# Retention attention and a routed expert layer on one core: 4096-byte x pieces, 512 KB weight loads, and a new deal of the front, the selections and the last steps

## The chip, the cores and the metric

One NeuronCore of a Trainium2 chip runs the whole program. The metric is device time in microseconds (us), the median of several executions.

## The reference

```
# attention: B=4, H=8, S=768, D=64, float32
for t in range(S):
    state = gamma * state + k[:, :, t] (outer) v[:, :, t]
    y[:, :, t] = scale * q[:, :, t] @ state
x = y as (B*S = 3072 tokens, H*D = 512)
# experts: 4 groups of 4, w1 (512, 1024) and w2 (1024, 512) each, float32
g_idx = argmax(x @ w_group);  e_idx = argmax(x @ w_expert[g_idx])
out[token] = softmax(g)[g_idx] * softmax(e)[e_idx] * relu(x @ w1[g, e]) @ w2[g, e]
```

Every token goes to one of 16 experts, which one is known only after its attention row is done.

## The kernel before

**The attention stage** runs 12 steps (i = 0 to 11), each with two batches of 128 tokens. A step has the score products of queries and keys (`score_mm`, into PSUM banks sh0 to sh3), the causal mask on VectorE (`score_mask`, tile pf), the product with the carried state (`state_out`), the product of pf with the scaled values (`value_out`; the scaling, tile vs, is `vprep` on GpSimd), the state update (`state_mm`, copied to V by ScalarE), the transposes of the next step's keys (`keys_mm`), and on VectorE the decay factors (`out_x`: xt = op * gx). The token logits of step i - 1 (`logits_mm`, copied to ls by ScalarE), the transposes of its xt into rows (`trans_mm`, copied to xr and written to the DRAM tensor xd), and the selection product that brings the logits into the bank log (line 326) come one step later. The scores of step i + 1 are made in step i, so that TensorE always has something between a product and its mask.

**Routing** (`route`) is a chain of some twenty small VectorE instructions for each four blocks of 128 tokens: maxima, one-hots (oh), a TensorE product that counts the ranks (lines 399 and 401), list slots and weights (src). GpSimd then scatters the token numbers into the experts' lists in DRAM (`enlist`, tensor meta). After the last step the order of the experts by load is computed (`order`, tile ord).

**The expert stage.** Experts 0 and 1 have an early list from the first half of the tokens; ua and va are those passes, ub and vb the rest of the same experts, us[0] to us[13] the other fourteen. A pass reads its list (tile mt), gathers rows of xd (tile xg), transposes them (`xtrans`, line 658), and splits x and the float32 weights wf into a float16 part and a bfloat16 rest: wh on ScalarE and wl on VectorE (`wsplit`, lines 616 and 618), xbh and xbl likewise. The first layer's products (line 681) go to banks hps, which `hh` (ScalarE) and `hl` (VectorE, line 689) empty, the second's (line 713) to yps. Early weight pieces of ua are split on GpSimd and ScalarE during the attention stage.

**What sets the order.** The program is written in its order by hand: the schedule is manual, each engine executes its instructions in the order in which the Python code records them, and the calls `beside(i, place)` and `extra(i)` put expert work into the attention steps. SyncE issues nearly all loads from one queue, in order. `NEXT` says which weight pieces of va are loaded at which step, `KEYED` which steps get their key rows by a load instead of transposes. Ahead of step 0, `attention` loads what a string names: q, k, v with a step number (A and B are halves), d for the decay table gx, w for the routing weights.

The lines that the change touches and what calls them:

## Time and profile before

| | us |
|---|---|
| median of 3 runs | 426.81 |
| lowest and highest | 423.11, 432.28 |
| profiled execution | 427.34 |
| its span in the trace | 425.6 |

The span runs from the first instruction to the end of the last write; the profiled execution's own time is 1.7 us above it. The profile page gives each engine's busy time; TensorE (PE) is busy for 404.0 us. Times in the rows further on are us from the span's start.

### The profile page before, as it was taken

How to read it: one execution, taken by the hardware profiler on the slowest of the kernel's cores; microseconds unless marked ns; L12 is line 12 of the kernel's file. 1: busy time of each engine (PE TensorE's matmuls, PEld its weight loads, DVE VectorE, ACT ScalarE, POOL GpSimd, SP SyncE). 2: the span in 40 equal slices, each digit the busy share in tenths (PEclk: the TensorE clock that was granted, in tenths of full speed). 3: DMA queues.
4: the chain of work that ended last, by engine and by line, in shares of the span. 5: the costliest groups of instructions: out<-in, count | busy, mean ns of one | idle time of the engine just before them, and what ended most of it. 6: DMA issues, size and time to landing. Idle time of an engine off the chain costs nothing.

```text
span 425.6 us, 13495 instructions
## 1 busy us (share of the span) xinstructions
PE 404.0 (95%) x5692; PEld 332.4 (78%) x5721; DVE 290.1 (68%) x473; ACT 222.8 (52%) x342; POOL 175.9 (41%) x153
## 2 busy tenths in 40 slices
PE   8899999999798999999999999999999999999991
PEld 4789888787675768585979788897978878879791
DVE  4455585578892557776889786867768777787620
ACT  2135336446541556646556665665766657667520
POOL 4445669748877022340508142351513405222001
PEclk9999999999999999999999999999999999999996
DMA  8999999997536867776776786978788797896001
GB/s 282 378 313 327 373 306 339 336 285 243 161 94 236 333 220 249 245 258 235 257 246 214 259 277 239 315 246 283 266 286 284 272 306 270 280 327 233 27 9 34
DMA packets 36913, 107.94 MB, mean 254 GB/s; under 512 B 13784, under 2 KB 13784, under 8 KB 29684
## 3 DMA queue, kind: packets, MB, share of 16 engines
q1 hardware_dynamic: 25908, 89.76, 61.9%
q0 software_dynamic: 10944, 17.31, 11.7%
q8 instruction: 45, 0.74, 0.7%
q14 instruction: 16, 0.13, 0.1%
HBM read 94.65 MB, written 13.77 MB: 255 GB/s over the span
## 4 chain that ended last, share of the span: by engine, by line
PE 58%; issue 26%; POOL 6%; DMA 4%; DVE 2%; SPq 1%; ACT 0%; POOLq 0%; DVEq 0%; ACTq 0%
PE hps L681 19%; PE yps L713 8%; PE yps L759 6%; PE yps L761 5%; PE op L291 5%; POOL out L814 4%; PE sh L227 3%; POOL xg L640 2%; PE op L278 2%; DMA gx<-dec 2%; PE sh L322 2%; PE tpx L658 2%; PE stp L253 2%; PE sh L310 2%; PE sh L212 1%
## 5 line engine op out<-in xcount | busy, mean ns | idle before, releaser
L618 DVE TENSOR_TENSOR wl<-wf,wh 128x1024 bf16<-128x1024 f32 x120 | 148.5, 1248 | 40.0 <-ACT wh L616 35.4
L681 PE MATMUL hps<-xbh,wh 128*128 128x128 f16 (+14 forms) x576 | 134.2, 245 | 0.9 <-ACT xr L329 0.9
L681 PE MATMUL hps<-xbl,wh 128*128 128x128 bf16 (+14 forms) x576 | 134.2, 245 | 0.3 <-issue 0.3
L616 ACT ACTIVATE wh<-wf 128x1024 f16<-128x1024 f32 (+1 forms) x136 | 133.5, 1002 | 1.8 <-DMA wf<-w1p 1.8
L681 PE MATMUL hps<-xbh,wl 128*128 128x128 f16 (+14 forms) x576 | 134.2, 245 | 0.1
L814 POOL DMA_INDIRECT out<-yo,mt x32 | 41.3, 1289 | 180.4 <-ACT yo L796 152.7
L681 PEld LDWEIGHTS <-wh 128*128 128x128 f16 x1152 | 102.5, 98 | 4.7 <-issue 1.9
L640 POOL DMA_INDIRECT xg<-xd,mt x32 | 52.5, 1641 | 26.3 <-DMA mt<-meta 17.4
L686 ACT ACTIVATE hh<-hps 128x256 f16<-128x256 f32 (+14 forms) x72 | 35.1, 488 | 52.3 <-PE hps L681 51.5
L761 PEld LDWEIGHTS <-wh 128*128 128x128 f16 x704 | 44.7, 98 | 21.0
L681 PEld LDWEIGHTS <-wl 128*128 128x128 bf16 x576 | 56.3, 98 | 1.1 <-issue 0.5
L239 DVE TENSOR_TENSOR pf<-sh,cst 128x512 f32<-128x512 f32 x48 | 30.8, 685 | 30.0 <-PE sh L227 10.3
L689 DVE SCALAR_TENSOR_TENSOR hl<-hps,hh 128x256 bf16<-128x256 f32 (+14 forms) x69 | 38.1, 553 | 16.7 <-ACT hh L686 14.2
L660 ACT ACTIVATE xbh<-tpx 128x512 f16<-128x512 f32 (+13 forms) x32 | 16.9, 527 | 47.2 <-PE tpx L658 47.1
L661 DVE TENSOR_TENSOR xbl<-tpx,xbh 128x512 bf16<-128x512 f32 (+13 forms) x32 | 19.2, 601 | 21.5 <-ACT xbh L660 21.5
L440 POOL DMA_INDIRECT meta<-src,slot x24 | 27.6, 1151 | 14.3 <-DVE src L394 7.1
L759 PE MATMUL yps<-wh,hh 128*128 128x512 f16 x88 | 33.4, 380 | 0.0
L759 PE MATMUL yps<-wh,hl 128*128 128x512 f16 x88 | 33.4, 379 | 0.0
L187 POOL TENSOR_TENSOR vs<-lv,cst 128x512 f32<-128x512 f32 x24 | 24.6, 1047 | 20.8 <-DMA lv<-qkv 10.9
L761 PEld LDWEIGHTS <-wl 128*128 128x128 bf16 x352 | 23.1, 98 | 10.4
L761 PE MATMUL yps<-hh,wl 128*128 128x103 f16 (+10 forms) x352 | 26.3, 197 | 1.2
L761 PE MATMUL yps<-hl,wh 128*128 128x103 bf16 (+10 forms) x352 | 26.3, 197 | 0.0
(146 smaller groups left out, 600.0 us busy)
## 6 DMA issues: line engine op xcount, KB each, us to landing
wf<-w1p SPq DMA_DIRECT2D x26, 1024.0 KB
wf<-w2p SPq DMA_DIRECT2D x26, 1024.0 KB
xd<-xr SPq DMA_DIRECT2D x12, 512.0 KB
lq<-qkv SPq DMA_DIRECT2D x11, 512.0 KB
lk<-qkv SPq DMA_DIRECT2D x11, 512.0 KB
lv<-qkv SPq DMA_DIRECT2D x11, 512.0 KB
wf<-w1p SPq DMA_DIRECT2D x16, 256.0 KB
wf<-w2p SPq DMA_DIRECT2D x16, 256.0 KB
```

The lines of the kernel that those rows point to most:

```text
L239: nc.vector.tensor_tensor(o, sc, tri, ALU.mult)
L440: i = nc.gpsimd.indirect_dma_start(out=self.metaf, out_offset=bass.IndirectOffsetOnAxis(ap=slot[:, c:c + 1], axis=0), in_=src[:, c, :], in ...
L616: nc.scalar.activation(u["wh"][i][:, cs], u["wf"][i][:, cs], AF.Copy)
L618: (eng or nc.vector).tensor_tensor(u["wl"][i][:, cs], u["wf"][i][:, cs], u["wh"][i][:, cs], ALU.subtract)
L640: nc.gpsimd.indirect_dma_start(out=xg[0:r, i, :], out_offset=None, in_=self.xd[0:n, :], in_offset=bass.IndirectOffsetOnAxis(ap=mt[0:r, i, ...
L681: nc.tensor.matmul(hv[:, a, 0:W], l[:, k, fs], r[:, k, 0:W], start=(n == 0), stop=(n == 11))
L686: nc.scalar.activation(hh[:, f, 0:W], hv[:, :, 0:W], AF.Relu)
L689: nc.vector.scalar_tensor_tensor(*rest)
L713: nc.tensor.matmul(ps[0:r, :], l[:, k, ts], m[k], start=(n == 0), stop=(n == 23))
L759: nc.tensor.matmul(big, h[:, k, 0:P], w[k], start=(n == 0), stop=(n == 23))
L761: nc.tensor.matmul(yv[:, d, 0:r], w[k][:, d * P:d * P + P], h[:, k, P:P + r], start=(n == 0 and d == 0), stop=(n == 23), skip_group_check= ...
L814: s = nc.gpsimd.indirect_dma_start(out=self.out, out_offset=bass.IndirectOffsetOnAxis(ap=mt[0:r, i, 0:1].bitcast(U32), axis=0), in_=yo[0:r ...
```

## The change

- The constants cst are loaded in two parts: 308 columns (masks and decay) at once and the remaining 263 (tile rest, routing constants) after the front loads. In the load string the decay table and v of step 1 come ahead of q and k of step 2.
- In steps 0 and 1 the scores of the next step are put behind `out_x`, and the keys of the next step are transposed into the bank log and sh0 instead of sh0 and sh1.
- A step's rows of x lie together in xd (token 256 i + 2 p + u), so xr goes out as 128 pieces of 4096 bytes instead of 256 of 2048; the host puts the output rows back in their order. Weight pieces of ua and va are 128 by 1024 (512 KB) instead of 128 by 512.
- The selection product is a function of its own, and in the steps whose keys are not transposed it is put off into the next step (`select_late`).
- The last steps: the last logits go to a bank of their own (tag sta), xr of the last step has its own buffer, one wl of va precedes the last route instead of four, three follow the held `hl` and stand ahead of `order`; the routing weights of the last route come ahead of its ranks; ua's fourth hps bank has the tag tra; xg1 is zeroed by ScalarE instead of GpSimd; in step 10 `vprep` precedes the gathers.
- `listed` has a new argument for the engine that reads the lists; no call gives it, so SyncE still reads them.

```diff
-NEXT = {9: (0, 4), 10: (4, 8), 11: (8, 12)}
+NEXT = {(9, 0): (0, 1), (9, 3): (1, 2), (10, 0): (2, 4), (11, 0): (4, 6)}
...
-    def logits_mm(self, i, bank):
+    def logits_mm(self, i, bank=None):
 
         nc, s = self.nc, self.st[i]
-        lt = self.sh[bank][:, 0:2 * P]
+        lt = self.pp.tile([P, 512], F32, name="lgt", tag="sta", bufs=1) if bank is None else self.sh[bank]
+        lt = lt[:, 0:2 * P]
...
-    def trans_mm(self, i):
+    def select_mm(self, i):
+
+        nc, s = self.nc, self.st[i]
+        for u in range(2):
+            a = LG + 20 * (i % 2 * 2 + u)
+            lg = self.log[:, a:a + 20]
+            nc.tensor.matmul(lg, s["ls"][:, u * P:u * P + P], self.rest[:, C_SEL:C_SEL + 20], start=True, stop=True)
+
+    def select_late(self):
+        if self.late is not None:
+            self.select_mm(self.late)
+            del self.st[self.late]
+            self.late = None
+
+    def trans_mm(self, i, pool=None, late=False):
 
         nc, s = self.nc, self.st[i]
...
-        for u in range(2):
-            a = LG + 20 * (i % 2 * 2 + u)
-            lg = self.log[:, a:a + 20]
-            nc.tensor.matmul(lg, s["ls"][:, u * P:u * P + P], self.cst[:, C_SEL:C_SEL + 20], start=True, stop=True)
-        xr = self.wp.tile([P, 2, DM], F32, name="xr", bufs=1)
+        if not late:
+            self.select_mm(i)
+        xr = (pool or self.wp).tile([P, 2, DM], F32, name="xr", bufs=1)
         for u in range(2):
             nc.scalar.activation(xr[:, u], self.sh[2 + u], AF.Copy)
-        g, c = divmod(i, NC)
-        xd = self.xd.rearrange("(b r) f -> r b f", r=S)[c * P:c * P + P, 2 * g:2 * g + 2, :]
-        nc.sync.dma_start(xd, xr)
+        xd = self.xd[2 * P * i:2 * P * i + 2 * P, :].rearrange("(p u) f -> p (u f)", u=2)
+        nc.sync.dma_start(xd, xr.rearrange("p u f -> p (u f)"))
...
+        if last:
+            yield from weights()
         yield "wait"
...
         if not last:
             yield "wait"
-        yield from weights()
+            yield from weights()
...
-        for o in "qB0 kB0 vA0 vB0 q1 k1 q2 k2 v1 d0 w0".split():
+        for o in "qB0 kB0 vA0 vB0 q1 k1 d0 v1 q2 k2 w0 c0".split():
             n, us = int(o[-1]), {"A": (0,), "B": (1,)}.get(o[1], (0, 1))
             if o[0] == "d":
                 self.decay_load()
+            elif o[0] == "c":
+                self.nc.sync.dma_start(self.rest, self.a_cst[:, C_REST:])
             elif o[0] == "w":
...
-            beside(i, -1)
             if not last:
                 self.vprep(i + 1)
+            beside(i, -1)
             if i == 3:
...
             if i:
-                scores(i + 1, 0)
+                if i > 1:
+                    scores(i + 1, 0)
+                if not last:
+                    self.select_late()
                 if i % 2 == 0:
                     self.route_steps(99, True)
                 self.state_out(i, 0)
+                self.select_late()
                 self.state_out(i, 1)
-                scores(i + 1, 1)
+                if i > 1:
+                    scores(i + 1, 1)
...
-            if i == 0:
-                scores(1, 0)
-                scores(1, 1)
             self.out_x(i)
+            if i < 2:
+                scores(i + 1, 0)
+                scores(i + 1, 1)
             if last:
                 self.route_steps(1, True)
             beside(i, 1)
             if not last:
-                self.keys_mm(i + 1)
+                self.keys_mm(i + 1, banks=(self.log, self.sh[0]) if i < 2 else None)
                 self.load("k", i + 4)
             if i:
-                self.trans_mm(i - 1)
-                del self.st[i - 1]
+                late = i + 1 in KEYED or i % NC == NC - 2
+                self.trans_mm(i - 1, late=late)
+                if late:
+                    self.late = i - 1
+                else:
+                    del self.st[i - 1]
...
+            ua["banks"] = ["big"] * 3 + ["tra"]
...
                 if place == 0:
                     if 2 <= i <= 9:
-                        for k in range(2):
-                            self.wload_part(ua, 2 * i - 4 + k)
-                    for k in range(*NEXT.get(i, (0,))):
-                        self.wload_part(va, k)
+                        self.wload_part(ua, i - 2)
                     if i == 10:
                         self.wsplit(va, 0, low=False)
-                        self.wsplit(va, 1, low=False)
-                    if last:
-                        self.wsplit(va, 0, high=False)
                 if place == 2:
                     if last:
-                        self.xtrans(ua, 'big', (0,))
-                        self.wsplit(va, 2, low=False)
+                        self.xtrans(ua, 'big', (0,), low=False)
+                        self.wsplit(va, 1, low=False)
                 if place == 1:
                     early(i - 1, 0, False)
                     if last:
-                        self.wsplit(va, 3, low=False)
+                        self.xlow(ua, 0)
+                if place == 3:
+                    if last:
+                        self.wsplit(va, 2, low=False)
...
-            nc.gpsimd.memset(self.xg[1], 0.0)
 
             last = NS2 - 1
-            self.logits_mm(last, 3)
-            for k in (1, 2, 3):
-                self.wsplit(va, k, high=False)
-            first(2)
-            self.trans_mm(last)
-            for k in range(12, 16):
+            self.logits_mm(last)
+            self.wsplit(va, 0, high=False)
+            self.trans_mm(last, self.yp)
+            for k in (6, 7):
                 self.wload_part(va, k)
             while self.todo:
                 self.enlist(*self.todo.pop(0))
...
             route = self.route(len(BATCHES) - 1)
             while next(route) != "wait":
                 pass
-            self.wsplit(va, 4, low=False)
-            self.wsplit(va, 5, low=False)
             self.held = []
             first(4)
+            self.wsplit(va, 3, low=False)
             next(route)
-            first(2)
+            first(4)
             for _ in route:
                 pass
             while self.todo:
...
             for h in self.held:
                 nc.vector.scalar_tensor_tensor(*h)
             self.held = None
-            self.xtrans(va)
+            self.xtrans(va, "sta")
+            for k in range(2):
+                nc.scalar.activation(self.xg[1][:, k], self.one, AF.Copy, scale=0.0)
+            self.wsplit(va, 4, low=False)
+            self.wsplit(va, 5, low=False)
             self.listed(ub)
             self.listed(vb)
+            for k in (1, 2, 3):
+                self.wsplit(va, k, high=False)
             self.steps.append(self.order())
             self.route_steps(99)
             assert not self.steps
-            self.wsplit(va, 4, high=False)
-            self.wsplit(va, 5, high=False)
+            for k in (4, 5):
+                self.wsplit(va, k, high=False)
```

Where it moves instructions. SyncE, the loads of the front, before:

```order
L177 DMA lq<-qkv 128x1024
L177 DMA lk<-qkv 128x1024
L177 DMA lq<-qkv 128x1024
L177 DMA lk<-qkv 128x1024
L177 DMA lv<-qkv 128x1024
L190 DMA gx<-dec 128x512
L879 DMA wr<-wr 128x4x20
```

and now:

```order
L178 DMA lq<-qkv 128x1024
L178 DMA lk<-qkv 128x1024
L191 DMA gx<-dec 128x512
L178 DMA lv<-qkv 128x1024
L178 DMA lq<-qkv 128x1024
L178 DMA lk<-qkv 128x1024
L904 DMA wr<-wr 128x4x20
L902 DMA rest<-cst 128x263
```

The decay table gx has moved ahead of q and k of step 2 and of v of step 1, v of step 1 ahead of q and k of step 2, and the second part of the constants behind wr.

TensorE at the end of the attention stage (log<-..,ls is the selection; sh the logits or the transposes of x; lgt the new bank), before:

```order
L322 MATMUL sh_108<-ident,xt 128x128 x4
L322 MATMUL sh_109<-ident,xt 128x128 x4
L326 MATMUL log<-cst,ls 128x20 x2
L310 MATMUL sh_109<-xt,wr 32x256 x4
L681 LDWEIGHTS wh
L681 MATMUL hps<-xbh,wh 128x128
```

and now:

```order
L338 MATMUL sh_110<-ident,xt 128x128 x4
L325 MATMUL log<-rest,ls 128x20 x2
L312 MATMUL lgt<-xt,wr 32x256 x4
L338 MATMUL sh_109<-ident,xt 128x128 x4
L338 MATMUL sh_110<-ident,xt 128x128 x4
L325 MATMUL log<-rest,ls 128x20 x2
L704 LDWEIGHTS wh
```

The last logits leave bank sh_109, into which the transposes just ahead of them were written, and the first layer of ua no longer stands between them and the last transposes and selection.

VectorE around the last route (r, slot: ranks to list slots; ex, eg, u, src: weights), before:

```order
L390 TENSOR_SCALAR u<-log 128x4
L392 SCALAR_TENSOR_TENSOR log<-log,u 128x4
L394 RECIPROCAL src_129<-log 128x4
L430 TENSOR_SCALAR rows_2147<-nb 1x1
L430 TENSOR_SCALAR rows_2149<-nb 1x1
L1081 SCALAR_TENSOR_TENSOR hl<-hps,hh 128x2x128 x3
L661 TENSOR_TENSOR xbl<-tpx,xbh 128x4x128
L461 TENSOR_TENSOR cnt<-nb,cst 1x16
L465 SCALAR_TENSOR_TENSOR key<-cnt,cst 1x16
L467 MEMSET key 1x1
```

and now:

```order
L425 TENSOR_TENSOR nb<-log,nb 128x16
L429 TENSOR_TENSOR r_2120<-log,oh 128x64
L431 TENSOR_REDUCE log<-r_2120 128x4
L434 CAST slot<-log 128x4
L445 TENSOR_SCALAR rows_2125<-nb 1x1
L445 TENSOR_SCALAR rows_2127<-nb 1x1
L1113 SCALAR_TENSOR_TENSOR hl<-hps,hh 128x2x128 x4
L683 TENSOR_TENSOR xbl<-tpx,xbh 128x4x128
L633 TENSOR_TENSOR wl<-wf,wh 128x1024 x3
L476 TENSOR_TENSOR cnt<-nb,rest 1x16
L480 SCALAR_TENSOR_TENSOR key<-cnt,rest 1x16
```

The weights have gone ahead of the ranks, all four hl are held until behind the route instead of three, and three wl of va, which stood ahead of the last route, now stand between it and `order` (cnt, key).

## Rows read from the trace of the kernel before

**Rows 1.** The profile page: the span, and each engine's busy time, share of the span and instructions.

```profile
span 425.6 us, 13495 instructions
PE 404.0 (95%) x5692; PEld 332.4 (78%) x5721; DVE 290.1 (68%) x473; ACT 222.8 (52%) x342; POOL 175.9 (41%) x153
```

**Rows 2.** Table of stretches, TensorE's granted clock and all engines; columns: stretch in us from the span's start, its length, busy time (and instructions) of PE, its weight loads PEld, DVE, ACT and POOL, granted clock, share of the DMA engines, GB/s. The rows: the front (steps 0 and 1), step 10, the end of attention with the first layer of ua, the fourteen other experts, the last write.

```profile
2.50:25.50 23.00, 20.82 (x404) 16.38 (x402) 11.12 (x21) 5.40 (x11) 11.27 (x16) 1.00 0.98 362
91.50:100.70 9.20, 8.53 (x184) 7.00 (x180) 8.19 (x19) 4.49 (x8) 4.16 (x4) 1.00 0.92 325
106.40:117.20 10.80, 7.63 (x121) 6.98 (x122) 9.43 (x28) 5.42 (x11) 9.45 (x8) 1.00 0.53 160
159.10:418.70 259.60, 256.01 (x3054) 212.53 (x3078) 189.85 (x233) 156.57 (x217) 82.26 (x53) 1.00 0.71 242
418.70:425.60 6.90, 0.00 (x0) 0.00 (x0) 0.00 (x0) 0.00 (x0) 0.00 (x0) 0.50 0.10 38
```

**Rows 3.** Timeline of the front and of step 2 (25.51 to 33.69) on TensorE, and of two other engines in the front; columns: start, time taken, engine, line, operation, output<-input, shapes, count, and in brackets the engine's idle time ahead of it and what ended it.

```profile
7.79 0.90 PE L227 MATMUL sh<-lq,lk 64*64 64x128 f32 x32 [0.67 <-DMA lk<-qkv]
12.36 1.57 PE L227 MATMUL sh<-lq,lk 64*64 64x128 f32 x64
17.57 0.40 PE L278 MATMUL op<-lq,V 64*64 64x128 f32 x2 [0.66 <-DVE xt L303]
25.51 0.90 PE L227 MATMUL sh<-lq,lk 64*64 64x128 f32 x32
...
31.43 1.09 PE L212 MATMUL sh<-ident,lk 128*128 128x128 f32 x8
33.69 0.90 PE L227 MATMUL sh<-lq,lk 64*64 64x128 f32 x32
...
16.00 2.04 POOL L187 TENSOR_TENSOR vs<-lv,cst 128x512 f32<-128x512 f32 x2 [5.52 <-DMA lv<-qkv]
13.33 2.48 DVE L239 TENSOR_TENSOR pf<-sh,cst 128x512 f32<-128x512 f32 x4 [3.29 <-PE sh L227]
16.73 1.29 DVE L303 TENSOR_TENSOR xt<-op,gx 128x512 f32<-128x512 f32 x2 [0.92 <-DMA gx<-dec]
```

**Rows 4.** DMA over the stretch 12 to 22, in which nearly all packets carry 4096 bytes, and under it over 100 to 118, in which nearly all large ones carry 2048; columns: queue, packets, MB, share of the 16 engines' time.

```profile
q1 hardware_dynamic: 1604, 3.71, 98.4%
...
q1 hardware_dynamic: 1540, 2.90, 55.2%
```

**Rows 5.** Timeline of TensorE in step 4, at the end of step 8 and at the end of step 10.

```profile
44.62 0.58 PE L227 MATMUL sh<-lq,lk 64*64 64x64 f32 x16 [0.80 <-issue]
82.18 0.62 PE L326 MATMUL log<-cst,ls 128*128 128x20 f32 x4 [0.21 <-ACT ls L315]
100.16 0.62 PE L326 MATMUL log<-cst,ls 128*128 128x20 f32 x4 [0.22 <-ACT ls L315]
```

**Rows 6.** Timeline of TensorE from the end of step 11 to the second layer of va.

```profile
107.35 0.64 PE L310 MATMUL sh<-xt,wr 128*32 128x256 f32 x8 [0.97 <-ACT xr L329]
112.91 0.22 PE L681 MATMUL hps<-xbh,wh 128*128 128x128 f16 x1 [0.90 <-ACT xr L329]
115.73 0.20 PE L399 MATMUL log<-oh,stri 128*128 128x80 bf16 x1 [1.32 <-DVE oh L374]
122.83 0.22 PE L681 MATMUL hps<-xbh,wh 128*128 128x128 f16 x1
128.19 0.38 PE L713 MATMUL yps<-wh,hh 128*128 128x512 f16 x1
132.53 0.66 PE L658 MATMUL tpx<-ident,xg 128*128 128x128 f32 x4 [1.58 <-DMA xg<-xd,mt]
```

**Rows 7.** Timeline of VectorE over the same stretch.

```profile
98.36 3.39 DVE L618 TENSOR_TENSOR wl<-wf,wh 128x1024 bf16<-128x1024 f32 x1
108.68 4.61 DVE L618 TENSOR_TENSOR wl<-wf,wh 128x1024 bf16<-128x1024 f32 x3
113.55 0.23 DVE L358 TENSOR_REDUCE m<-log 128x20 f32<-128x80 f32 x1
115.46 0.22 DVE L374 TENSOR_TENSOR oh<-log,go 128x64 bf16<-128x64 f32 x1
118.22 0.18 DVE L394 RECIPROCAL src<-log 128x4 f32<-128x4 f32 x1
122.83 2.35 DVE L618 TENSOR_TENSOR wl<-wf,wh 128x1024 bf16<-128x1024 f32 x2
125.10 0.42 DVE L689 SCALAR_TENSOR_TENSOR hl<-hps,hh 128x256 bf16<-128x256 f32 x1
```

**Rows 8.** Timeline of GpSimd over the same stretch (vs is the scaling of values; meta a scatter to the lists, xg a gather).

```profile
96.17 1.08 POOL L640 DMA_INDIRECT xg<-xd,mt  x1 [6.63 <-DMA mt<-meta]
98.62 2.05 POOL L187 TENSOR_TENSOR vs<-lv,cst 128x512 f32<-128x512 f32 x2
112.19 1.95 POOL L440 DMA_INDIRECT meta<-src,slot  x1 [0.30 <-PE hps L681]
114.45 0.98 POOL L440 DMA_INDIRECT meta<-src,slot  x1 [0.30 <-issue]
122.98 1.93 POOL L440 DMA_INDIRECT meta<-src,slot  x1 [0.30 <-DVE ord L490]
129.08 1.05 POOL L640 DMA_INDIRECT xg<-xd,mt  x1 [2.88 <-DMA mt<-meta]
```

More of the change, by code (lines that the diff above doesn't have):

```diff
@@ L340, in route @@
         c0, n = BATCHES[i]
-        cst = self.cst
+        cst = self.rest
         def t(name, *shape, dt=F32):
@@ L451, in order @@
     def order(self):
-        nc, rp, cst = self.nc, self.rp, self.cst
+        nc, rp, cst = self.nc, self.rp, self.rest
         V = nc.vector
@@ L494, in items @@
     def items(self):
-        nc, rp, cst = self.nc, self.rp, self.cst
+        nc, rp, cst = self.nc, self.rp, self.rest
         V = nc.vector
@@ L618, in wsplit, with listed @@
             (eng or nc.vector).tensor_tensor(u["wl"][i][:, cs], u["wf"][i][:, cs], u["wh"][i][:, cs], ALU.subtract)
-    def listed(self, u, group=None):
+    def listed(self, u, group=None, eng=None):
         nc, tc, bp = self.nc, self.tc, self.bp
@@ L670, in layers @@
         for f2 in range(4):
-            ps = pp.tile([P, 512], F32, name="hps", tag="big", bufs=3)
+            tag = u.get("banks", ["big"] * 4)[f2]
+            ps = pp.tile([P, 512], F32, name="hps", tag=tag, bufs=3 if tag == "big" else 1)
             hv = ps.rearrange("p (a t) -> p a t", a=2)
@@ L952, in attention @@
                 self.route_steps(99, True)
+            if i == 1:
+                self.nc.vector.tensor_copy(self.stri, self.rest[:, C_STRI:C_STRI + P])
             entries(4 if last else 2 if i in (8, 10) else 1)
@@ L1017, in beside @@
                 last = i == NS2 - 1
+                for k in range(*NEXT.get((i, place), (0,))):
+                    self.wload_part(va, k)
                 if place == -1 and i == 10:
@@ L1200 @@
     r = run_bass_kernel_spmd(nc, [arrays], core_ids=[0])
-    return r.results[0]["out"]
+    out = r.results[0]["out"].reshape(B // 2, NC, P, 2, DM)
+    return np.ascontiguousarray(out.transpose(0, 3, 1, 2, 4)).reshape(NT, DM)
```

49 lines of the change are left out of this document (28 added, 21 removed).

## Prediction

> **What bounds the kernel now.** I read the busy times first, then the table of stretches, then the waits of TensorE. [...] In the fourteen late experts it idles 3.6 of 259.6 us, and the change leaves their order alone, so that stretch keeps its length; the 6.9 us of the last write stay too. What can be had lies ahead of 136 us: 2.2 idle us in the front, 0.7 in step 10, 3.2 between 106.4 and 117.2 [rows 2], 1.58 at the gather of ub [rows 6]. A busy TensorE is not always a working one: matmuls held up inside a group count as busy. So I price stretches by comparing one with another that does the same work.
>
> **The front.** Step 2 runs from 25.51 to 33.69, 8.18 us, without a named wait. The stretch from 12.36 to 25.51, 13.15 us, has the same work plus one more pair of scores (1.57) and one more set of key transposes (1.09): 10.84 us. So 2.3 us are lost there, of which the trace names 0.66, the wait for `out_x`, which itself waits for the decay table until 16.73 [rows 3]. In the new order of loads 1 MB (q and k of step 2, 128 x 1024 x 4 bytes each) and v of step 1 (0.52 MB) no longer stand ahead of the table: 1.57 MB at the 377 GB/s that a stretch of 4096-byte packets reached (3.71 MB in 98.4% of 10 us) [rows 4] are 4.2 us, so it lands near 12.5, when value_out of step 0 has just ended. v of step 1 comes 1.05 MB less 0.26 MB earlier, 2.1 us: its scaling starts at 13.9 instead of 16.00 [rows 3], and value_out of step 1, which now stands ahead of the next scores, needs it only near 15.7. What is late next are the masks: `out_x` (1.29) now precedes them on VectorE, and sh0, sh2 and sh3 come free one mask (0.62, from 2.48 for four) [rows 3] after another; I count 0.4 us of such waits, from 0 to 1.2. The bank log for the first key transposes takes away the wait for sh0 at no cost, since the selection comes 2 us later. The constants shrink by 263 of 571 columns, 135 KB, 0.36 us at that rate, in front of the load for which TensorE waits 0.67 us at 7.79 [rows 3]: 0.36. The sum of the front is 2.3 - 0.4 + 0.36, **2.3 us**, from 1.0 (the named 0.66 and 0.36 alone) to 2.7.
>
> **Late selections.** At the ends of steps 8 and 10 the selection waits 0.21 and 0.22 us for ls [rows 5]. Put off behind the next scores or half of `state_out`, it finds ls ready: **0.4 us**, from 0 to 0.4. Its consumer, the route's first maximum, still stands behind masks.
>
> **The end of attention.** I keep the clock of before. TensorE is through with the selection of step 10 at 106.38 (107.35 less 0.97) [rows 6]. The last logits now have their own bank, so the 0.97 goes; logits (0.64), transposes (1.09 as for keys) [rows 3] and selection end near 108.6, and 48 products of ua's first layer follow, half of the 5.36 us that va's 96 take from 122.83 to 128.19 [rows 6]: 111.3. The 0.90 at 112.91, for xr that waited for its last write, goes with the new buffer.
> VectorE comes free at 108.68. Before, three wl (4.61) stood ahead of the last route, which began at 113.55 and had oh at 115.68, 2.13 later [rows 7]. Now one wl does, 1.54: oh comes at 112.35. TensorE waits 1.0 us for it in place of 1.32. From there to va's first layer it took 7.1 us (115.73 to 122.83) [rows 6], now 1.34 more for the 24 products that went behind the ranks: 120.8.
> But nothing was taken off VectorE. From oh to the first hl of va it took 9.84 us (115.68 to 125.52) [rows 7]; now it has one more hl (0.42) and three wl (1.18 each, half of 2.35): 13.8, so that hl ends at 126.1. The fourth bank of va's first layer needs that hl. TensorE has three banks done at 124.8 and waits 1.3 us: a new wait. The first layer ends at 127.5 instead of 128.19, 0.7 sooner.
> Then the gather of ub. Before, xg came at 132.53, 7.6 us after the last scatter to the lists ended (122.98 + 1.93) [rows 6, 8]. TensorE will want it 2.6 us after 127.5, at 130.1. The slots are ready at 115.1, since the whole chain from oh to src took 2.72 (115.68 to 118.40) [rows 7]. GpSimd is freed of the 2.05 of vs behind the gathers, for which it sat idle 6.63 us ahead of them [rows 8], and of the zeroing of xg1; so it starts four scatters at 108.9, when src is there. One costs 0.98 + 0.30, beside a wl 1.95 + 0.30 [rows 8]. Four with one slow one and a wl of ua (about 1.2) bring it to 116.2; the last four, two of them beside the three moved wl, take 7.0: 123.2 instead of 124.91. So xg comes at 130.8 and TensorE waits 0.7 instead of 1.58, 0.9 less. The sum of the end is 0.7 + 0.9, **1.6 us**; from -0.5 (all four scatters slow, wl at 1.54) to 4.8 (all four waits gone, if VectorE keeps up).
> [...] The rows: a wl took 3.39 us at 98.36 while vs ran on GpSimd from 98.62 to 100.67, and a scatter 1.95 beside a wl, 0.98 without [rows 7, 8]. [...] By the rows a scatter pays 0.97 once, which is in the sum; if GpSimd found no gap between three wl in a row, it would pay more, which is a rival below.
>
> **The larger pieces.** The 6.3 MB of xr and 8.4 MB of early weights moved at 2.90 MB in 55.2% of 18 us, 292 GB/s of full use, against 377 [rows 4]: 50 us of the queues become 39. TensorE names hardly a wait for them (xr's is counted above), so I price them at **0**, from 0 to 3: waits like the 0.80 at 44.62 have no releaser in the profile [rows 5] and might be of the loaded queues. The list reads for ua come sooner, for which only GpSimd waits. The rest (renumbered tokens, zeroing on ScalarE, four hps banks for ua) I price at nothing: the scatters and gathers keep their number and size, and ScalarE is busy 5.42 of 10.8 us there [rows 2].
>
> **The sum** is 2.3 + 0.4 + 1.6 = 4.3 us. The profiled execution took 427.34, so it gives 423.0; it lies 0.5 above the median of the three runs, and against that median I forecast **422.5 us**, 1.0% less.
>
> **Rivals.**
> 1. *The queues were the hidden cause.* Step 10 takes 9.2 us though it has no keys to transpose, against 8.18 in step 2, with only 0.67 of it idle [rows 2, 3]; if such stretches are held up by queues busy for 0.92 of their time, the larger pieces give 3 us more, and VectorE's end of the chain comes forward too: 4.3 + 3 + 1.6, 417.9. Against it: behind the 0.67 at 7.79, no wait of TensorE in [rows 3, 5, 6] names a load, only the gather. [...]
> 2. *The scatters are shut out during all three wl*, 3.5 us instead of 1.9 for two: xg at 132.4, a wait of 2.3 instead of 0.7: gain 2.7, 424.1. For it: 3.39 us of a wl beside vs. Against: the scatter at 112.19 ran among three wl in a row (108.68 to 113.29) too, and took 1.95.
> 3. *The front's gain is given back*, because the queues, full from 2.5 to 100 us (shares 0.98 and 0.92) [rows 2], cannot feed a TensorE that runs 2 us ahead: gain 2.0, 424.8. Against it: loads are issued two steps ahead.
> 4. *VectorE falls behind and the kernel is slower.* Five wl now stand between the last slots and the first hl of va. At 3.39 [rows 7] instead of 1.18 each they would take 11.0 us more: hl at 137.1, the first layer's end at 138.4 instead of 128.19, +10.2, less the 1.58 that nobody then waits for and the 2.7 of the front and selections: +5.9, 432.7. It decides from 0.9 us more for each wl. Against it: that price was paid beside a 2 us GpSimd operation, and there only scatters of 1 us run.
>
> **How the numbers follow.** Chances: the forecast 0.52, rival 1 0.17, rival 2 0.11, rival 3 0.12, rival 4 0.08. Faster by over 2% (below 418.3) is rival 1 and little of the rest: 0.15; slower by over 2% needs more than rival 4: 0.03; within 2%, about what a measurement of this kernel can tell from no change, 0.82. The sum's ends are 1.0 + 0 - 0.5 = 0.5 and 2.7 + 0.4 + 4.8 + 3 = 10.9, which would not all meet; the range goes from rival 1 with a little more, 416.5, to near the lower end, 426.5.
>
> **What would show it.** Right: step 2 starts 2 to 2.5 us sooner; no waits for xr at the last logits; a wait of about 1 us for oh and a new one for hl in va's first layer; ub's gather waited for by under 1 us; from 136 us on all of it shifted by one amount. Wrong: a decay table that lands after 14 us, steps 8 to 10 shorter than 8.2, 9 and 9 us (rival 1), or a wl over 2 us behind the last slots (rival 4).

## Result and profile after

The changed kernel took 428.65 us (median of 22 runs, 425.49 to 430.41) where the kernel before, on the same chip, took 426.93 (22 runs): ratio 1.0052, 95% interval 1.0030 to 1.0074. I had forecast 422.5. The profiled execution took 429.59 us. Executions over 1.5% above the fastest of their kernel (two of one variant took 832 and 1055 us) stay out of the ratios, here and below, but not out of the medians.

The page, and the table of stretches cut as in [rows 1, 2] (the same columns; front, step 10, end of attention, fourteen other experts, last write):

```profile
span 427.9 us, 13485 instructions
PE 406.4 (95%) x5721; PEld 333.1 (78%) x5721; DVE 287.1 (67%) x473; ACT 225.1 (53%) x344; POOL 174.2 (41%) x152
```

```profile
2.50:25.50 23.00, 20.88 (x404) 16.26 (x402) 11.13 (x21) 5.83 (x11) 11.60 (x16) 1.00 0.99 366
95.70:104.30 8.60, 7.58 (x185) 6.66 (x180) 6.48 (x19) 3.64 (x7) 5.96 (x7) 1.00 0.94 326
109.70:120.40 10.70, 8.65 (x131) 7.88 (x130) 8.29 (x36) 5.61 (x11) 5.94 (x6) 1.00 0.40 156
161.40:420.90 259.50, 257.35 (x3079) 212.55 (x3078) 189.81 (x233) 156.50 (x217) 82.26 (x53) 1.00 0.71 242
420.90:427.90 7.00, 0.00 (x0) 0.00 (x0) 0.00 (x0) 0.00 (x0) 0.00 (x0) 0.61 0.10 39
```

The fourteen experts and the last write last as long as before; the difference lies ahead of them. TensorE's timeline there, which answers to [rows 3, 5, 6]:

```profile
21.52 1.11 PE L228 MATMUL sh<-lq,lk 64*64 64x128 f32 x40 [0.81 <-issue]
24.02 1.25 PE L338 MATMUL sh<-ident,xt 128*128 128x128 f32 x8 [0.37 <-DVE pf L240]
25.57 0.34 PE L228 MATMUL sh<-lq,lk 64*64 64x128 f32 x6
...
45.98 0.88 PE L228 MATMUL sh<-lq,lk 64*64 64x64 f32 x27 [1.55 <-issue]
52.94 0.30 PE L228 MATMUL sh<-lq,lk 64*64 64x64 f32 x4 [0.96 <-issue]
84.10 0.82 PE L254 MATMUL stp<-vs,kk 128*64 128x64 f32 x15 [2.22 <-issue]
97.64 0.62 PE L325 MATMUL log<-rest,ls 128*128 128x20 f32 x4 [1.02 <-DVE slot L434]
...
113.23 0.59 PE L325 MATMUL log<-rest,ls 128*128 128x20 f32 x4 [0.94 <-DVE src L407]
117.62 0.20 PE L414 MATMUL log<-oh,stri 128*128 128x80 bf16 x1 [1.11 <-DVE src L407]
131.28 0.22 PE L704 MATMUL hps<-xbh,wh 128*128 128x128 f16 x1 [1.04 <-DVE hl L712]
132.62 0.38 PE L736 MATMUL yps<-wh,hh 128*128 128x512 f16 x1
135.62 0.55 PE L673 MATMUL tpx<-ident,xg 128*128 128x128 f32 x3 [0.25 <-DMA xg<-xd,mt]
```

The waits that I meant to remove are gone: none for `out_x`, for ls or for xr. Step 2 still starts at 25.57 (with the scores of step 3, as before), where before it started at 25.51 [rows 3]. In place of the old waits stand waits that name no releaser: 5.5 us of them in this table, against 1.3 before, of which [rows 5] shows the longest, 0.80. Behind the 2.22 us wait more is lost. In the next table (columns as in [rows 2]) the granted clock is 0.50 from 84.50 on:

```profile
81.88:84.10 2.22, 0.00 (x0) 0.00 (x0) 1.46 (x3) 0.00 (x0) 1.97 (x2) 1.00 1.01 388
84.50:87.90 3.40, 3.40 (x29) 2.14 (x29) 0.00 (x0) 1.60 (x4) 3.08 (x4) 0.50 0.61 114
```

At 0.50 the eight transposes from 85.87 on took 1.97 us; the eight from 75.33 on, at 1.00, took 1.04. Half speed for 3.4 us is, as an estimate, 1.7 us more. That the wait brought the fall isn't shown.

**Where these waits stand.** The counts in the table of stretches tell it. I cut it from 0 to just before each wait ends, first for the kernel after, then for the kernel before at its waits at 44.62 and 79.35:

```profile
0.00:21.50 21.50, 18.88 (x347) 13.81 (x348) 9.83 (x19) 5.44 (x9) 10.33 (x22) 1.00 0.91 334
0.00:45.96 45.96, 41.32 (x857) 33.83 (x858) 24.65 (x56) 15.08 (x28) 20.69 (x32) 1.00 0.92 330
0.00:52.92 52.92, 47.33 (x985) 38.77 (x985) 27.15 (x60) 18.04 (x34) 27.09 (x38) 1.00 0.92 329
0.00:84.08 84.08, 76.23 (x1623) 64.48 (x1623) 49.09 (x124) 29.84 (x59) 49.15 (x59) 1.00 0.94 323
```

```profile
0.00:44.60 44.60, 40.75 (x857) 33.76 (x857) 23.99 (x53) 14.61 (x28) 20.63 (x32) 1.00 0.94 329
0.00:79.33 79.33, 75.06 (x1622) 64.21 (x1623) 47.61 (x122) 29.06 (x59) 47.11 (x57) 1.00 0.95 330
```

Products and weight loads together are 695, 1715, 1970 and 3246. The steps between them are 1020, 255 and 1276: about 4, 1 and 5 times 255. The table leaves out TensorE's semaphore instructions. Counted in the records themselves, with those, the waits end at instruction 705, 1729, 1985 and 3265, which is 193 + 256 k each time, and before at 1729 and 3265. So these waits stand at the bounds of blocks of 256 instructions. The DMA view of the whole trace has a queue `instruction` (q8) of that grain: 45 packets, 0.74 MB, for 11,503 records of TensorE, and 45 times 256 is 11,520. These are three stretches of 0.2 us, 2.4 us ahead of the ends of the waits at 45.98, 52.94 and 84.10 (queue, packets, MB, share of the 16 engines):

```profile
q1 hardware_dynamic: 23, 0.07, 90.8%
q8 instruction: 1, 0.02, 30.8%
...
q1 hardware_dynamic: 19, 0.08, 94.4%
q8 instruction: 1, 0.02, 30.4%
...
q1 hardware_dynamic: 20, 0.07, 92.2%
q8 instruction: 1, 0.02, 28.9%
```

In each, one packet of 16,384 bytes starts on the queue `instruction`; shared by 256 instructions that would be 64 bytes each. This gives theory F (fetch): the packet brings TensorE its next 256 instructions; with the data's queues full (shares of 0.91 to 0.94 up to these waits) it starts late, and TensorE stands at its bound until about 2.4 us after that start (2.37 to 2.47 in these three). I measured that distance for the first 15 blocks of all 20 traces of this study. Of 300 none is under 2.16 us, and 154 lie between 2.16 and 2.65, 10 of 15 in the changed kernel; in the fourteen experts, where the queues are used for 0.71, it is 5 to 20 us, mostly near 10. In the kernel before too 10 of its 15 lie below 2.65: by theory F it was bound there as well, if briefly: its waits at 44.62 and 79.35 are 0.80 and 0.15 us. The longest wait at one bound in any of the 20 traces is 2.77 us. Which DMA engine carries a packet stands in no view: that instructions and data get in each other's way there is the theory's assumption.

The rival S (schedule): these waits are something of the program at those places, a bank or a buffer whose record is missing, or the new order of the front, the selections or the last steps.

### The profile page after: what moved, and what is told of

Its sections match the earlier page's. It is cut to its first block, busy times and chain, and to the rows that moved or that the text cites. A ratio compares the mean times of both kernels' runs of the same rounds, so it can differ in the third digit from the quotient of the medians.

```text
span 427.9 us, 13485 instructions
## 1 busy us (share of the span) xinstructions
PE 406.4 (95%) x5721; PEld 333.1 (78%) x5721; DVE 287.1 (67%) x473; ACT 225.1 (53%) x344; POOL 174.2 (41%) x152
## 4 chain that ended last, share of the span: by engine, by line
PE 59%; issue 23%; POOL 7%; DVE 5%; DMA 3%; SPq 1%; POOLq 0%; ACT 0%; DVEq 0%; ACTq 0%
PE hps L704 19%; PE yps L736 8%; PE yps L782 6%; PE op L292 5%; PE yps L784 5%; POOL out L837 4%; PE sh L228 4%; POOL xg L655 3%; PE sh L338 2%; PE op L279 2%; PE tpx L673 2%; PE stp L254 2%; DMA gx<-dec 2%; PE sh L312 1%; PE sh L213 1%
## 5 line engine op out<-in xcount | busy, mean ns | idle before, releaser
L633 DVE TENSOR_TENSOR wl<-wf,wh 128x1024 bf16<-128x1024 f32 x120 | 145.1, 1220 | 39.8 <-ACT wh L631 39.6
L712 DVE SCALAR_TENSOR_TENSOR hl<-hps,hh 128x256 bf16<-128x256 f32 (+14 forms) x68 | 37.6, 555 | 15.7 <-ACT hh L709 15.4
L455 POOL DMA_INDIRECT meta<-src,slot x24 | 26.1, 1088 | 21.0 <-DVE src L407 10.3
L782 PE MATMUL yps<-wl,hh 128*128 128x512 bf16 x88 | 33.4, 379 | 0.0
L228 PE MATMUL sh<-lq,lk 64*64 64x64 f32 (+1 forms) x768 | 23.3, 253 | 3.8 <-issue 3.3
```

The costliest lines, as they stand in the source:

```text
L228: nc.tensor.matmul(self.sh[2 * u + par][64 * half:64 * half + 64, cs], kT[rs, ks:ks + 64], qT[rs, cs], start=True, stop=True, skip_group_c ...
L633: (eng or nc.vector).tensor_tensor(u["wl"][i][:, cs], u["wf"][i][:, cs], u["wh"][i][:, cs], ALU.subtract)
L712: nc.vector.scalar_tensor_tensor(*rest)
L782: nc.tensor.matmul(big, h[:, k, 0:P], w[k], start=(n == 0), stop=(n == 23))
```

## Experiments

Every ratio is to the kernel before on the same chip, with its 95% interval.

**Does the wait follow the block?** Three warming products fewer, 48 tiny ones more ahead of the first load:

```
-WARM = 9
+WARM = 6
...
+        for i in range(48):
+            nc.tensor.matmul(warm[0:1, 0:1], one[:, 0:1], one[:, 0:1], start=True, stop=True)
```

> The changed kernel with 96 tiny TensorE instructions more (48 products of one column) and 3 of the 9 warming products less, all ahead of the first load, so that every instruction behind stands 90 places later in the instruction stream. Theory F: the waits without a releaser stay at instruction 193 + 256 k of the stream, so at products that are 90 instructions earlier in the program than before; the time moves by up to 2 us either way. Rival S (a missing record of a semaphore, a bank or a buffer): they stay at the same products, the scores of step 4 and 5 and the states of step 8; time 428.6 within 0.7.

432.75 us, 1.0108 (1.0048 to 1.0167). TensorE's three longest waits from 40 us on, and the counts up to two of them:

```profile
43.32 0.44 PE L230 MATMUL sh<-lq,lk 64*64 64x128 f32 x8 [0.67 <-issue]
49.24 0.45 PE L256 MATMUL stp<-vs,kk 128*64 128x64 f32 x8 [1.35 <-issue]
94.45 0.27 PE L340 MATMUL sh<-ident,xt 128*128 128x128 f32 x1 [2.43 <-issue]
```

```profile
0.00:43.30 43.30, 40.84 (x857) 34.33 (x858) 23.02 (x48) 14.64 (x28) 20.66 (x32) 1.00 0.95 325
0.00:49.22 49.22, 45.41 (x985) 38.65 (x986) 27.81 (x60) 14.88 (x28) 23.03 (x35) 1.00 0.95 334
```

Count 1715 and 1971 again, though the program stands 90 instructions further back. The products are others: the first wait stands in the first half of that step's scores instead of the second, the second at a state instead of a score. The third ends at instruction 3777, which is 193 + 256 k again. S is out as the cause of these waits.

**Do full queues make the packets late?** Of expert 0's weight pieces only 64 of 1024 columns are loaded (in the kernel before 32 of 512), the tile is zeroed by ScalarE:

```
+        if u["e"] == 0 and h == 0:
+            for n in range(4):
+                self.nc.scalar.activation(u["wf"][i][:, n * 512:n * 512 + 512], self.one, AF.Copy, scale=0.0)
+        cs = slice(h * 1024, h * 1024 + (64 if u["e"] == 0 else 1024))
```

> The changed kernel, but of each 512 KB weight piece of expert 0 only 64 of 1024 columns are loaded in the attention stage (0.03 MB instead of 0.52, 8 pieces, 3.9 MB less in steps 2 to 9) and the rest is zeroed by ScalarE, so that expert 0 computes with other weights; everything else is unchanged. Theory F: the backlog shrinks, the fetches start earlier, the products at packet bounds no longer follow 2.4 us behind them, the waits without a releaser in steps 2 to 9 go (3 to 5 us of the changed kernel), and steps 2 to 8 shorten: 423 to 426. Rival S: 428.6 within 0.7, the waits stay.

> The kernel before with 1/16 of the columns of expert 0's weight pieces loaded in the attention stage and the rest zeroed by ScalarE (so expert 0 computes with other weights), as in the same cut of the changed kernel. With the queues relieved, the two kernels can be compared where the fetch of instructions binds less. Theory F: before gains less than the changed kernel did from this, since its fetches were less late, and the changed kernel then stands where the local gains put it, 1 to 3 us below this one: this one 427 to 429. Rival S (order of the changed kernel costs 1.5 to 2 us by itself): this one 1.5 to 2 us faster than the cut changed kernel, near 424.5.

After with the cut: 426.56, 0.9953 (0.9917 to 0.9988), 1.0% below the changed kernel. Before with the cut: 425.68, 0.9935 (0.9908 to 0.9962). Blocks that begin within 2.65 us of their packet's start: 3 of 15 in either, from 10. The same stretch, first after, then after with the cut:

```profile
26.00:100.00 74.00, 68.02 (x1526) 59.54 (x1518) 44.96 (x126) 29.39 (x60) 47.34 (x45) 0.98 0.92 302
```

```profile
26.00:100.00 74.00, 71.43 (x1619) 63.17 (x1612) 47.40 (x130) 38.86 (x81) 52.94 (x52) 1.00 0.85 269
```

93 products more in the same time, with a DMA share of 0.85 in place of 0.92. The kernel before, without and with the cut:

```profile
26.00:100.00 74.00, 71.53 (x1601) 62.46 (x1592) 48.95 (x131) 30.57 (x65) 46.68 (x45) 1.00 0.97 325
```

```profile
26.00:100.00 74.00, 71.64 (x1634) 63.79 (x1627) 47.86 (x132) 41.27 (x84) 51.37 (x49) 1.00 0.88 279
```

So most of the 93 is what the changed kernel had lost against before, which got through 1601 products with the queues at 0.97: the mean share alone doesn't say how late the packets start. Theory F holds for where the waits stand and for their shrinking when bytes go: those without a releaser are 5.5 us in the changed kernel and 2.0 with the cut (TensorE's waits from 10 to 108 us, one profile of each). That the whole gain came by the fetch isn't shown: before gained 0.65%, 2.8 us, though its listed waits without a releaser were only 1.3 us. And two of my side expectations were wrong. Before did gain, and with the cut the changed kernel was to lie 1 to 3 us below it, but the two cannot be told apart.

**Where the front's gain went.** Steps 3 and 4 take over the q, k and v of earlier steps, so that six loads are gone from 10 to 25 us:

```
+        if i in (3, 4):
+            st[name] = self.st[i - (2 if name == "v" else 3)][name]
+            return
```

> The changed kernel, but steps 3 and 4 load no q, k and v and compute with those of steps 0, 1 and 2 that are still in place (six loads, 3.1 MB, gone from the queues between 10 and 25 us; their tokens come out otherwise). Only steps 0 to 2 are compared. Theory F: with less behind which they stand, the fetches of the front start earlier, the product at the third packet bound no longer waits, and step 2 starts 1.5 to 2.3 us sooner than at 25.57, which is what I forecast for the front. Rival S (the front has another limit, such as masks or VectorE): step 2 starts at 25.6 within 0.4.

> The kernel before with the same six loads left out of steps 3 and 4. Here the decay table still lands behind q and k of step 2 and v of step 1, so the wait for it stays. Theory F: step 2 starts less than 1 us sooner than at 25.51, and the distance to the changed kernel with the same cut is the gain of the new front without the fetch, 1 to 2.3 us. Rival S: both start at 25.5.

The first scores of step 2, after with the cut and before with the cut:

```profile
24.23 0.43 PE L231 MATMUL sh<-lq,lk 64*64 64x128 f32 x8
```

```profile
25.92 0.45 PE L230 MATMUL sh<-lq,lk 64*64 64x128 f32 x9
```

1.7 us apart, where with all loads they were level. This rests on one execution of each; in it the front did most of what I had worked out for it. In the full program TensorE ran into the block bound at 20.71, waited 0.81 there, and at 21.5 was level with before (692 instructions by then, 695 after). In the other direction, the old front in the new kernel:

```
-        for o in "qB0 kB0 vA0 vB0 q1 k1 d0 v1 q2 k2 w0 c0".split():
+        for o in "qB0 kB0 vA0 vB0 q1 k1 q2 k2 v1 d0 w0 c0".split():
```

> The changed kernel with the order of before in the front: loads of q and k of step 2 ahead of v of step 1 and the decay table, scores of steps 1 and 2 and the key transposes in their old places and banks (the constants still in two parts). Theory F: steps 0 and 1 take the same time as with the new front, because the products at the packet bounds wait 2.4 us behind fetches that start at the same moments: step 2 begins at 25.5 within 0.4, the total within 0.7 of the changed kernel. If the new front were the loss (loads in a worse order for the steps behind): 2 us below it. If the new front gave what I forecast: 2 us above it.

435.6, 1.0120 (1.0048 to 1.0192); `value_out` of step 2 starts at 28.4, after at 28.3, as theory F had it. The total is 0.7% (within 0.75) above the changed kernel, which I had written down as the sign of a front that gives its gain; but in its trace the time is lost behind the front, 21.5 us from `value_out` of step 9 to that of step 11, so the total settles nothing here. Over all traces in which the loads of the front are whole `value_out` of step 2 starts at 27.4 to 28.6 with the new front (12 traces, mean 28.1) and at 28.0 to 31.0 in the kernel before and its variants (5 traces, mean 29.4): the profile of before that I read was its best front. In two of the others the wait for `out_x` had grown to 1.7 us and the clock fell beside it.

**Which part loses.** Larger pieces in the kernel before, both and each alone, and small ones in the changed kernel:

> The kernel before with 4096-byte x pieces and 512 KB weight pieces alone (the weights of va in the steps of before). If long packets delay the fetches: 428.5 to 430, waits without a releaser longer than the 1.3 us of before in sum. If only bytes count: 427 within 0.7. The prediction's rival 1 (small pieces as a hidden cause): 424.

> The kernel before with 4096-byte x pieces alone (layout of xd, token numbers, order of the output). Both larger pieces together cost 0.9% there. If the x writes are what does it: ratio 1.006 to 1.01. If the weight pieces: within 0.3% of before.

> The kernel before with 512 KB weight pieces alone, in the steps of before. If packets of 4096 bytes of the weights are what delays the fetches (they are issued at the start of a step together with q and v): ratio 1.005 to 1.01. If the x writes: within 0.3% of before.

> The changed kernel with 2048-byte x pieces (token numbers, layout of xd and order of the output as before) and 256 KB weight pieces at the same places; front, selections and last steps as changed. Theory F (fetch): in both traces TensorE's instructions come in transfers of 16,384 bytes, 256 instructions, on a queue of their own; the product at which a new packet begins starts 2.3 to 2.5 us after the packet's transfer started, at nearly every packet of the attention stage, and the waits without a releaser stand exactly there. The transfers start late because the DMA engines have a backlog of data packets. If long packets of 4096 bytes (193 ns each against 106) are what makes the backlog costly, small pieces give 425 to 427 and a mean delay of the fetches below that of the changed kernel. If the amount of bytes is what counts, 428.6 within 0.7. Rival S (schedule): front, selections or last steps are what costs, pieces nothing: 428.6 within 0.7, with the waits at the same products.

Both: 432.67, 1.0090 (1.0054 to 1.0127). The x pieces alone 430.03, 1.0018 (0.9989 to 1.0046); the weight pieces alone 431.24, 1.0038 (1.0005 to 1.0071). In the kernel before the larger pieces cost 2.3 to 5.4 us; which of the two does it isn't settled. The changed kernel without them: 430.23, 1.0035 (1.0002 to 1.0068), hardly less than with them, so something else loses too. The selections in their own steps (`late = False`):

> The changed kernel with the selections at the ends of steps 4, 8, 9 and 10 again in their own step instead of the next one. If the late selections are what costs (1.0 us of wait ahead of the one in step 10, for the route's last read of the bank log): 1 us or more below the changed kernel, and waits of 0.2 us for ls instead. Theory F: the 1.0 goes but what is gained there is given back at the next packet bounds: within 0.7 of the changed kernel.

431.87, 1.0072 (1.0040 to 1.0103): no gain. The 1.02 us wait for slot in step 10 goes, 0.20 for oh and 0.31 for ls come. Holding back one load a step, q of step i + 3 behind the write of x:

> The changed kernel with the load of q for step i + 3 issued behind the write of x at the end of step i instead of in its middle, so that up to 0.5 MB less stands in the queues at a time, most of all in steps 0 to 2. Nothing else moves. Theory F with the backlog as the reason that fetches start late: the fetches of the front and of steps 3 to 6 start earlier, step 2 begins up to 2 us sooner, and the total is 1 to 3 us below the changed kernel, unless q itself comes too late (a wait that names the load). If the backlog is not the reason: no change within 0.7.

432.51, 1.0089 (1.0052 to 1.0127): no gain either, against what theory F had led me to expect. That the total in the queues matters, and not where in a step one load is issued, would fit, but isn't shown.

What was left were the deal of va's weights and, in step 10, the scaling ahead of the gathers:

```
-NEXT = {(9, 0): (0, 1), (9, 3): (1, 2), (10, 0): (2, 4), (11, 0): (4, 6)}
+NEXT = {(9, 0): (0, 2), (10, 0): (2, 4), (11, 0): (4, 6)}
```

> The changed kernel with the weights of va dealt as before: both pieces of step 9 at its start, instead of one at its start and one at its end. In the traces so far, steps 9 to 11 (from value_out of step 9 to that of step 11) take 20.1 to 21.6 us in five of the variants with the new schedule and 15.3 to 17.4 in all with the old one. Theory N: the piece moved to the end of step 9 now stands with the two of step 10 and the two gathers in one bunch of 1.6 MB, behind which the fetch and the gathers wait: these steps shorten to 17 or less and the total falls by 2 to 4 us below the changed kernel (430.8 beside a before of 428.6). Theory V (the scaling of values ahead of the gathers makes GpSimd's indirect transfers run in one row of four): no change from this.

> The changed kernel with the gathers of step 10 ahead of the scaling of values again. Theory V: the four indirect transfers of GpSimd come in two pairs again, the broken groups of TensorE beside them (five products each 0.73 us) go, steps 9 to 11 take 17 us or less, the total falls by 2 to 4 us. Theory N: no change.

> The changed kernel with both of these undone: the deal of va's weights and the order of gathers and scaling as before. If the two together are what steps 9 to 11 lose: 426.5 to 428.5 beside a before of 428.6, steps 9 to 11 in 17 us or less. If neither: 430.8 within 1, and the loss there comes from the late selections or the last steps.

> The changed kernel with small x pieces and small weight pieces, the deal of va's weights and the order of gathers and scaling as before; what is left of the change are the front, the late selections and the last steps. If larger pieces (0.6 to 0.9% in the kernel before) and the deal in steps 9 and 10 are the losses: 1 to 2 us below before, which is what the last steps gave in the traces (1.2 us). If the loss lies in the rest: 1 us or more above before.

Old deal: 428.17, 1.0002 (0.9957 to 1.0047). Old order of scaling: 428.28, 1.0040 (1.0001 to 1.0078). Both: 428.76, 1.0015 (0.9970 to 1.0060). Both, and small pieces: 425.00, **0.9955** (0.9921 to 0.9990). Of the first three, each with larger pieces, the old deal lies lowest, but all three intervals reach into that of the changed kernel, and the order of the scaling alone shows nothing. From `value_out` of step 9 to that of step 11 the new deal took 15.7 to 21.6 us in nine traces with full weights (over 20 in six of them), the old deal 15.3 to 19.3 in nine. With the new deal three pieces of 512 KB were issued in one row ahead of the gathers of step 10. Last, the same without late selections, and the changed kernel itself once more:

> The changed kernel with small x pieces and small weight pieces, the deal of va's weights and the order of gathers and scaling as before, and the selections in their own steps: of the change, the front and the last steps are left. Without the late selection its wait of 1.0 us in step 10 goes (0.2 to 0.3 us for ls comes back in four steps). If that wait counts: 0 to 1 us below the same kernel with late selections, whose ratio to before is 0.9955. If what is gained is given back at the next packet bound: no difference within 0.4%.

> The changed kernel itself, unchanged, once more, for a second profile and for times beside the variants' before. Its first profile had 15.7 us from value_out of step 9 to that of step 11, where the variants with the same deal of va's weights had 20.1 to 21.6. If the deal is what costs there, this profile has 17 to 22; if 15.7 is what the changed kernel takes, the loss lies in steps 4 to 8 alone. Ratio 1.003 to 1.0075.

With the front and the last steps alone left of the change: 424.24 us, **0.9932** (0.9897 to 0.9966), faster than both kernels. The changed kernel again: 428.84, 1.0035 (1.0001 to 1.0069). Its second profile has 17.4 us in steps 9 to 11, the bound at instruction 3265 again, and behind the wait for slot a clock of 0.50:

```profile
84.43 0.68 PE L254 MATMUL stp<-vs,kk 128*64 128x64 f32 x15 [2.77 <-issue]
96.46 0.62 PE L325 MATMUL log<-rest,ls 128*128 128x20 f32 x4 [1.02 <-DVE slot L434]
```

```profile
97.30:100.70 3.40, 3.40 (x70) 3.26 (x64) 1.32 (x7) 0.00 (x0) 2.79 (x3) 0.50 1.01 325
```

A chain of ratios, each kernel with one part more, leads to the whole:

| left of the change | ratio | step |
|---|---|---|
| front and last steps | 0.9932 | -0.7% |
| and late selections | 0.9955 | +0.2% (within 0.5) |
| and larger pieces | 1.0015 | +0.6% (within 0.6) |
| and the new deal and order of scaling (the changed kernel) | 1.0052 | +0.4% (within 0.5) |

The ends are settled. A middle step is hardly larger than its own uncertainty, and with the second measurement of the changed kernel, 1.0035, the last one is only 0.2%. For the pieces the kernel before agrees (0.9%), for the deal a second pair does (1.0035 against 0.9955 with small pieces). But the parts don't simply add: with the new deal kept, small pieces gave 0 to 0.2% (1.0035, against 1.0035 and 1.0052).

## Why the prediction was wrong

**The step that failed** is the pricing of the larger pieces at 0, from 0 to 3 us of gain. I compared what the queues carry (292 against 377 GB/s) and took "TensorE names hardly a wait for them" to mean that the queues could only help. They can also hurt: with expert 0's loads cut, TensorE's waits without a releaser fell from 5.5 to 2.0 us, which theory F puts down to instructions that came sooner. The trace of before had the sign of it, the 0.80 us wait at 44.62 without a releaser [rows 5], which I mentioned as perhaps of the loaded queues, and then bounded on the side of a gain alone. Measured: +0.6% with the old deal and +0.9% in the kernel before, 2.5 to 4 us. The forecast that the queues would be done sooner failed as well. The kernel before with both larger pieces:

```profile
26.00:100.00 74.00, 70.01 (x1606) 62.37 (x1604) 45.88 (x128) 31.35 (x65) 47.73 (x47) 1.00 0.97 326
```

That is 326 GB/s at a share of 0.97, where before had 325 at 0.97 with the small ones: the size of the pieces didn't raise the rate, and 292 against 377 compared stretches that differ in more than it. How the larger pieces cost time stays open. That packets of 4096 bytes make the fetch later isn't shown: its packets start on average 115 instructions ahead of their block in before and 125 with both larger pieces, and 101 and 129 in two traces of the changed kernel itself. The one profile with both larger pieces in the kernel before, of its fastest execution, has only 1.7 us of waits without a releaser.

**The deal of va's weights** had no price at all, since I counted bytes and not what they bunch with. With the order of the scaling it cost 0.2 to 0.8%, by which pair is taken.

**The front, 2.3 us:** its steps came as forecast: the decay table landed at 12.75 (forecast 12.5), the mask waits were 0.21 and 0.37 (0.4 in sum), TensorE waited 0.49 for k in place of 0.67 (0.31). In the pair of profiles none of it arrived: at 21.5 the wait at the block bound had taken back what there was. With the loads cut 1.7 of it showed, and over many traces 1.3. Rival 3 had the place right, full queues that give the front's gain back, and the carrier wrong: the 0.81 us at 20.71 ends at instruction 705 and names no load, which by theory F is a wait for instructions, not data.

**Late selections, 0.4:** ls was no longer waited for. But the selection writes the bank log, which VectorE's route was still reading, and in step 10 it waited 1.02 for slot, where before `state_out` had waited 0.45 for it and the selection 0.22 for ls [rows 5]:

```profile
93.05 0.99 PE L278 MATMUL op<-lq,V 64*64 64x128 f32 x27 [0.45 <-DVE slot L419]
```

In four traces the clock fell behind that wait of 1.02. The same bank brought 0.94 at 113.23: I had moved the last selection forward and not asked what still read its bank. By the ratios the late selections cost 0.2% (within 0.5), so neither the gain nor a loss is shown.

**The end of attention, 1.6:** from `value_out` of step 11 to the transposes of ub it took 29.0 instead of 30.2, 1.2 less (29.2 on average in the 14 traces of the new schedule, 30.3 in the six of the old). The new waits for hl and xg came as forecast, 1.04 (forecast 1.3) and 0.25 (0.7; by [rows 6] TensorE wants xg 2.8 us behind the start of the second layer, where I took 2.6, which makes it 0.5). That a wait of 1.11 stands where I had put 1.0 for oh is luck. VectorE's rows:

```profile
116.03 0.23 DVE L387 TENSOR_TENSOR oh<-log,go 128x64 bf16<-128x64 f32 x1
117.39 0.18 DVE L407 RECIPROCAL src<-log 128x4 f32<-128x4 f32 x1
```

oh was there at 116.26, before TensorE was through with ua's products (116.5). The product at 117.62 waited for src, the end of the weights that the change had put ahead of the ranks; they work in the bank log, into which the product writes. In all 14 traces of the new schedule it starts 0.05 us behind src. And from 136 us on not all of it shifted by one amount: from 144.07 to 156.34 the changed kernel took 12.27 us for what took 13.06 before (140.97 to 154.03). Half of the 14 traces have that gain, why isn't known. Rivals 2 and 4 are out by VectorE's and GpSimd's rows:

```profile
122.32 3.49 DVE L633 TENSOR_TENSOR wl<-wf,wh 128x1024 bf16<-128x1024 f32 x3
```

```profile
122.86 1.53 POOL L455 DMA_INDIRECT meta<-src,slot  x1 [0.30 <-issue]
124.69 1.97 POOL L455 DMA_INDIRECT meta<-src,slot  x1 [0.30 <-issue]
```

Three wl took 1.16 each, and the scatters beside them 1.5 and 2.0. Rival 1 is refuted by sign. Front and end together, forecast at 3.9 us, gave 2.9 (1.5 to 4.4) where they stand alone. Their size was right, in part by luck; all the rest of the change, forecast to gain 0.4, cost 5.1 us (1.0052 against 0.9932; 4.4 by the second measurement of 1.0035).

**Still open:** why most traces of the new schedule take some 2 us more in steps 2 to 9 even where pieces, deal or selections are as before (mean 60.1 from `value_out` of step 2 to that of step 9 in 12 traces, against 58.1 in four of the old schedule), and how the fastest kernel, whose own profile has 5.9 us of waits without a releaser, is faster all the same. One profile is one draw: executions of a kernel spread over 3 to 10 us, and the bounds at which TensorE waits change from draw to draw.

## What to carry to other kernels

A wait of TensorE without a releaser is worth a count of the instructions up to it. Here nine such waits, in three kernels, end at 193 plus a multiple of 256, and what the front had saved was gone behind the one at 20.71. Then the thing to price is what stands in the DMA queues at that moment, on both sides of zero, for every edit that moves or enlarges a load: 3.9 MB less of loads took 1.0% off the changed kernel. When a product or a chain of another engine is moved, look who else uses its bank there: three new waits of about 1 us here were for the bank log.

## What the hardware showed that I had not expected

- None of 300 blocks of 256 TensorE instructions began sooner than 2.16 us after its packet on the queue `instruction` started, and in the changed kernel's first profile its packet started up to 5.0 us after TensorE had entered the block before.
- In 12 of 20 traces the granted clock fell to 0.50 ahead of 140 us, for 3.4 us (once 6.8), by estimate 1.7 us of lost work for each 3.4; in all but one this came within a microsecond of a wait of 0.9 to 2.8 us. Other such waits passed with the clock at 1.00, the one of 2.77 us among them.
- In five traces TensorE worked in groups of about five products each 0.73 us, for 2 to 5 us, while GpSimd's indirect transfers ran in step 10. All five have the new deal and are among the six that took over 20 us from `value_out` of step 9 to that of step 11. The old front in the new kernel shows it; the cause is not known:

```profile
99.19 0.45 PE L228 MATMUL sh<-lq,lk 64*64 64x64 f32 x5 [0.27 <-issue]
99.93 0.35 PE L228 MATMUL sh<-lq,lk 64*64 64x128 f32 x5 [0.29 <-issue]
100.67 0.45 PE L292 MATMUL op<-pf,vs 128*64 128x128 f32 x4 [0.39 <-issue]
101.40 0.49 PE L292 MATMUL op<-pf,vs 128*64 128x128 f32 x5 [0.28 <-issue]
```
